# One transformer block on one core: query features scaled on one side only, written into padded rows at once; a new hand-written order with freely placed weight loads

## The chip, the cores and the metric

The kernel runs on one core of one Trainium2 chip. The metric is the device time of one execution in microseconds (us). TensorE (PE) multiplies matrices into PSUM, VectorE (DVE) and ScalarE (ACT) read PSUM and compute elementwise, GpSimd (POOL) computes elementwise on SBUF, and SyncE (SP) issues DMAs. ACT can issue DMAs too. Each engine works through its own list of instructions in order and waits on semaphores for the others.

## The reference

```python
def _A_ref(x, wqkv, w_phi, wo):                     # S = 2048, D = 640, H = 32, Dh = 20
    q, k, v = split(x @ wqkv)
    pq = einsum("bhsd,hdf->bhsf", q, w_phi)
    pk = einsum("bhsd,hdf->bhsf", k, w_phi)
    phi_q = concatenate([softmax(pq), softmax(-pq)], axis=-1)
    phi_k = concatenate([softmax(pk), softmax(-pk)], axis=-1)
    kv = einsum("bhsf,bhsd->bhfd", phi_k, v)
    z  = einsum("bhsf->bhf", phi_k)
    num = einsum("bhqf,bhfd->bhqd", phi_q, kv)
    den = einsum("bhqf,bhf->bhq", phi_q, z) + 1e-6
    return (num / den) @ wo
def _B_ref(x, w_gate, w_up, w_down):                # F = 1536
    return ((x @ w_gate) * (x @ w_up)) @ w_down
h = x + _A_ref(_layernorm(x), ...)
h2 = h + _B_ref(_layernorm(h), ...)
```

All inputs are bfloat16. The attention is linear: the sums over all keys (`kv`, `z`) must be complete before the first query can be divided.

## The kernel before, in words

The 2048 rows are 16 tiles of 128. For each tile t these operations exist, each with the name that the text uses (line numbers of the profile):

- **L1s, L1a, L1l, L1e, xn, xt**: first layer norm (L427 to L452) and the transposed tile, by PE for tiles 0 to 3 (L461), by a DMA transpose from SP's queue for the others (L470).
- **K, V, Q**: products of 128x640x640, ten matmuls of 320 columns each (L483). The feature matrix `w_phi` is folded into the K and Q weights first: WT (transposes of the K weights, L391), F1 and F0 (folds, L410), with their copies WTe, Fe1, Fe0 (L250).
- **Kx, Ks, Kr, Ke, Kn**: K features. Two ACT exponentials of 640 columns (plus and minus, L495), a DVE sum over 64 groups of 20 (L499), ACT `Ln` and `Exp` for the reciprocal (L502, L504), a POOL product over 1280 columns (L519).
- **KV**: eleven matmuls per tile that add up `kv` and `z` in PSUM (L527). After the last, **KVe** (L534) masks the result into `KVm`.
- **Qx, Qs, Qr, Qe, Qn**: the same for Q; POOL's Qn (L550, L554) scales all 1280 columns and writes them into rows of 11 blocks of 128 (`ph`). **qT** (L561) transposes these rows by DMA.
- **N**: numerator and denominator of a tile, twelve matmuls (L575), since block 5 is cut in two at a PSUM bank. **dd, rd, o** (L586, L588, L591) add 1e-6, take the reciprocal, and multiply. **oT** (L595) transposes, **O** multiplies by `wo` (L601), **h** adds `x` (L605).
- **L2s, L2a, L2v, L2r, hc, hT**: second layer norm, and its transpose by DMA (L628).
- **U, g, u, D, y, w**: the gated block in five groups of rows (256, 512, 512, 512, 256): gate and up products (L643), ACT copy (L648), DVE product (L651), down product (L662), residual (L674), store (L676). The first group, U0, needs tiles 0 and 1 only.

The order is written out by hand in a table, `PLAN`: per operation a key, a choice of engine where there are two, and buffer slots. Each engine runs its operations by rising key; the keys set the order only, and semaphores do the rest. `PACE` holds the weight loads behind the transposes of late tiles. PSUM has eight banks; a K, V, Q, N or O result takes two.

Around the change the orders are these. DMA issues at the start, all by SP: x0 w5 wk0 wk1 x1 wk2 x2 wk3 wk4 x3 wv1 wv0 wv2 x4 wv4 wv3 x6 x14 x8 x10 x12 (x of one or two tiles, wk and wv in fifths of 160 KB). Later: SP issues xt15 wg0 xt13 wo0 wu1 wu4 wo2 wd3 xt14 and seven more weights, ACT wg1 wu2 wd0. PE has finished eight Q products when the last KV ends; then come Q9 N1 N0 Q11 Q12 Q13 N2 Q14 N3 Q10 O1 O0 N5 Q8 N6 O2 Q7 N15 O3 N9 N4 and U0. SP, from the first transpose of an `o` tile to that of h tile 0: oT1 oT0 qT6 qT4 oT2 qT15 oT3 qT9 hT1 hT0.

Of the kernel before, what the change touches and what calls it, by code (L numbers as in the profile page):

```python
# [34 lines left out]
BW = [120 * g for g in range(10)] + [1152]  # L35
# [9 lines left out]
NSLOTS = {"psum": 8, "xn": 4, "ek": 7, "va": 8, "SR": 4, "ph": 4, "phT": 6, "o": 3, "oT": 4, "gt": 4, "hh": 2, "out": 3,  # L45
# [3 lines left out]
x0:0.7 w5:1.18:1 wk0:1.66:1 wv0:5.98:1 wk1:2.14 wv1:5.5 wk2:3.1:1 wv2:6.46:1 wk3:4.06 wv3:7.9 wk4:4.54:1 wv4:7.42:1 x1:2.62 x2:3.58 x3:5.02:1 x4:6.94  # L49
x6:8.38 x8:9.34 x10:9.82 x12:10.3 x14:8.86 wqt0:32.637 wqt1:35.357 wqt2:29.917 wqt3:27.197 wqt4:39.852 wo0:44.412 wo2:45.852 wd0:45.168:1 wd1:51.052  # L50
wd2:50.092 wd3:46.332 wg0:42.572 wu0:49.132 wg1:42.572:1 wu1:44.892 wg2:49.612 wu2:43.825:1 wg3:48.652 wu3:48.172 wg4:50.572 wu4:45.372 id0:2.41
gl0:0.7 eps:0.95 id1:2.93 gla0:3.77 glb0:4.21 gla4:2.19 glb4:3.33 gla1:1.97 glb1:3.55 gla2:4.43 glb2:4.85 gla3:2.71 glb3:3.99 va1:1.15 phz:6.025
mk0:4.65 mk1:5.07 mk2:5.775 mk3:6.925 mk4:7.325 zero:0.7 warm0:1.08::0 warm1:1.51 warm2:1.94 warm3:2.37 warm4:2.8 warm5:3.23 warm6:3.66 warm7:4.09
warm8:4.52 warm9:4.74 Ph0:4.717:1 Ph1:5.32 Ph2:4.36:1 WT0:4.96::1 WTe0:5.573:1 WT1:5.239::0 WTe1:5.788:1 WT2:6.114::3 WTe2:6.812:1 WT3:7.024::6
WTe3:8.16 WT4:7.725::7 WTe4:8.578:1 F1_0:6.394::4 Fe1_0:7.035:1 F1_1:6.709::0 Fe1_1:7.658 F1_2:7.41::2 Fe1_2:8.282:1 F1_3:8.763::0 Fe1_3:9.435
F1_4:9.387::6 Fe1_4:10.058:1 L1s0:3.021 L1a0:4.021 L1s1:5.992 L1a1:7.23 L1s2:7.34 L1a2:10.427 L1s3:8.997 L1a3:10.317 L1s4:10.537 L1a4:13.497
L1s5:11.357 L1a5:14.537 L1s6:13.607 L1a6:14.647 L1s7:12.177 L1a7:14.427 L1s8:19.637 L1a8:22.207 L1s9:16.397 L1a9:22.097 L1s10:14.757 L1a10:20.567
L1s11:15.577 L1a11:20.457 L1s12:25.657 L1a12:33.07 L1s13:30.22 L1a13:32.96 L1s14:29.4 L1a14:35.53 L1s15:33.18 L1a15:35.42 L1l0:4.311 L1e0:4.741
L1l1:8.905 L1e1:9.335 L1l2:10.717 L1e2:11.689 L1n2:12.199 L1n3:11.999 L1l4:14.996 L1e4:15.839 L1n4:16.349 L1n5:16.749 L1n6:16.149 L1n7:16.549
L1l8:23.514 L1e8:23.974 L1n8:24.884 L1n9:24.484 L1n10:24.684 L1n11:24.284 L1l12:35.85 L1e12:36.28 L1n12:37.279 L1n13:37.479 L1n14:36.879 L1n15:37.079  # L60
xn0:5.073::0 xt0:5.753::2 xte0:6.412 xn1:9.817::0 xt1:10.517::0 xte1:11.066 xn2:12.997::0 xt2:13.801::2 xte2:14.372 xn3:13.036:1:1 xt3:14.08::3
xte3:15.216 xn4:17.809:1:2 xt4:21.977 xn5:17.717::1 xt5:19.257 xn6:19.146:1:3 xt6:20.617 xn7:17.217::0 xt7:17.897 xn8:26.814:1:2 xt8:31.277
xn9:31.04::0 xt9:33.997 xn10:25.861:1:1 xt10:28.557 xn11:25.157::0 xt11:25.837 xn12:37.812::1 xt12:38.492 xn13:39.771:1:3 xt13:43.052 xn14:37.661:1:0
xt14:46.812 xn15:39.732::2 xt15:41.212 V0_0:9.115::2 V0_1:9.702 V0_2:10.245 V0_3:11.339 V0_4:11.611 Ve0:12.412::0 K0_0:8.004::4 K0_1:8.492 K0_2:9.973
# [12 lines left out]
Kn12:51.973 KV12:62.675 V13:51.405::0 Ve13:53.034::0 K13:49.504::2 Kx13_0:51.2::2 Kx13_1:52.033 Ks13:52.867::0 Kr13:54.472 Ke13:55.335 Kn13:56.691
KV13:69.782 V14:67.066::0 Ve14:69.077::2 K14:58.285::0 Kx14_0:60.33::1 Kx14_1:61.164 Ks14:61.997::1 Kr14:64.047 Ke14:64.497 Kn14:66.676 KV14:70.098
V15:61.317::4 Ve15:63.424::1 K15:47.515::4 Kx15_0:49.143::0 Kx15_1:49.977 Ks15:51.123::2 Kr15:52.723 Ke15:53.657 Kn15:54.332 KV15:70.413 KVe0:71.259
KVe1:70.999 F0_0:44.896::0 Fe0_0:45.648 F0_1:46.884::0 Fe0_1:47.469:1 F0_2:42.592::0 Fe0_2:43.823:1 F0_3:45.211::4 Fe0_3:46.272 F0_4:49.189::0  # L80
# [4 lines left out]
Qs4:69.287::1 Qr4:71.074 Qe4:71.937 Qn4:76.661::0 qT4:79.989::1 Q5:62.991::0 Qx5_0:64.647::3 Qx5_1:65.51 Qs5:66.344::2 Qr5:68.214 Qe5:69.7
Qn5:71.577::1 qT5:74.269::0 Q6:64.349::2 Qx6_0:66.134::4 Qx6_1:66.967 Qs6:67.8::0 Qr6:69.85 Qe6:70.3 Qn6:74.119::2 qT6:78.489::2 Q7:86.856::4
Qx7_0:88.485::2 Qx7_1:89.318 Qs7:110.524::0 Qr7:112.124 Qe7:112.574 Qn7:112.934::0 qT7:115.855::1 Q8:83.561::4 Qx8_0:85.19::0 Qx8_1:86.023
Qs8:101.317::1 Qr8:103.114 Qe8:103.66 Qn8:104.387::0 qT8:108.296::5 Q9:70.729::0 Qx9_0:72.357::0 Qx9_1:73.191 Qs9:76.05::2 Qr9:77.951 Qe9:78.814
Qn9:81.745::3 qT9:85.709::0 Q10:79.024::4 Qx10_0:80.652::6 Qx10_1:81.485 Qs10:91.885::0 Qr10:93.568 Qe10:94.114 Qn10:94.474::0 qT10:98.369::1
Q11:72.773::6 Qx11_0:74.414::1 Qx11_1:75.247 Qs11:77.66::0 Qr11:79.587 Qe11:80.451 Qn11:87.029::1 qT11:95.509::0 Q12:74.131::0 Qx12_0:75.871::3  # L90
Qx12_1:76.704 Qs12:95.909::1 Qr12:97.509 Qe12:98.164 Qn12:98.524::2 qT12:101.216::3 Q13:75.489::4 Qx13_0:77.327::4 Qx13_1:78.191 Qs13:80.622::1
Qr13:82.222 Qe13:82.672 Qn13:84.287::0 qT13:89.929::2 Q14:77.19::6 Qx14_0:78.964::5 Qx14_1:79.827 Qs14:99.435::0 Qr14:101.035 Qe14:101.485
Qn14:101.845::1 qT14:105.436::4 Q15:68.424::2 Qx15_0:70.45::2 Qx15_1:71.314 Qs15:72.147::3 Qr15:73.814 Qe15:74.264 Qn15:79.203::1 qT15:82.849::3
N0:72.43::2 dd0:73.757::1 rd0:74.247 o0:75.299::1 oT0:77.129::1 O0:81.86::6 h0:83.545 L2s0:85.117 L2a0:87.037 L2v0:89.571 L2r0:110.394 hc0:87.327::1
# [142 lines left out]
def build_graph():  # L237
# [662 lines left out]
```

## Time and profile before

| | before |
|---|---|
| median of 3 runs | 278.28 us (278.23 to 278.49) |
| the profiled execution | 276.56 us, of which its span 274.8 us |
| granted TensorE clock | 0.999 |
| PE, DVE, ACT, POOL busy | 266.0, 172.3, 113.2, 88.6 us |
| HBM read, written | 11.00 MB, 2.62 MB |

The span runs from the first to the last instruction; all times within the trace count from its start. Matmuls are pipelined: the time of one (299 ns for 320 columns) is a latency, and the rate is read from a long run of them. A group's idle time is the time that its engine had nothing to do just before it, with what ended that.

### The profile page before, as it was taken

The numbers are of one execution on the slowest core, as the hardware profiler recorded it, in microseconds if no ns is written. First come the engines' busy times: TensorE is split into PE (matmuls) and PEld (weight loads), VectorE is DVE, ScalarE is ACT, GpSimd is POOL, SyncE is SP. The second block draws the span as 40 slices with busy tenths as digits, with TensorE's granted clock in tenths as the row PEclk, the third lists the DMA queues.
The fourth block names the chain that finished last, engine by engine and source line by source line (L and its number), as shares of the span: only waits on it lengthen the run. The fifth ranks groups of instructions, "written<-read, shape, count | busy, mean of one in ns | idle before, by whom it ended". The sixth has DMA issues, their size and how long they took to land.

```text
span 274.8 us, 5227 instructions
## 1 busy us (share of the span) xinstructions
PE 266.0 (97%) x2119; PEld 176.7 (64%) x2119; DVE 172.3 (63%) x319; ACT 113.2 (41%) x240; POOL 88.6 (32%) x105
## 2 busy tenths in 40 slices
PE   7899999899999799999999999999999999999995
PEld 3676777677777587764455787665554467544773
DVE  5899999767789979987576337433365122323432
ACT  4899887678985444303242232003012310033000
POOL 7016999979998438240000000000000000000000
PEclk9999999999999999999999999999999999999999
DMA  6944758999689789867522100331002001100011
GB/s 167 317 144 95 98 110 174 302 294 341 141 147 176 146 141 186 163 74 160 52 47 49 26 0 2 84 50 48 25 2 48 0 0 50 52 0 2 24 48 57
DMA packets 66600, 27.77 MB, mean 101 GB/s; under 512 B 57744, under 2 KB 65296, under 8 KB 66576
## 3 DMA queue, kind: packets, MB, share of 16 engines
q1 hardware_dynamic: 65888, 26.15, 44.8%
q10 hardware_dynamic: 688, 1.28, 1.9%
q8 instruction: 17, 0.28, 0.4%
q14 instruction: 7, 0.06, 0.1%
HBM read 11.00 MB, written 2.62 MB: 50 GB/s over the span
## 4 chain that ended last, share of the span: by engine, by line
PE 84%; DMA 7%; DVE 4%; SPq 3%; issue 0%; DVEq 0%; ACT 0%
PE ps L643 34%; PE ps L483 22%; PE ps L662 17%; PE ps L601 7%; DMA xnT<-xn 3%; SPq L284 2%; PE ps L575 2%; DMA Wp<-in_A_wqkv_dram 2%; DMA scratch<-o 2%; DVE SR L499 2%; PE ps L527 1%; DMA out_dram<-Wp 1%; DVE o L591 1%; SPq L595 0%; DVE Wp L674 0%
## 5 line engine op out<-in xcount | busy, mean ns | idle before, releaser
L643 PE MATMUL ps<-xnT,Wgu 128*128 128x512 bf16 (+1 forms) x600 | 107.0, 336 | 1.2 <-DMA xnT<-xn 1.0
L643 PEld LDWEIGHTS ps<-xnT,Wgu 128*128 128x128 bf16 x600 | 58.0, 98 | 44.2 <-DVE ev L651 1.2
L648 ACT ACTIVATE gt<-ps 128x512 bf16<-128x512 f32 (+1 forms) x60 | 30.7, 512 | 101.9 <-PE ps L643 89.0
L483 PE MATMUL ps<-Wp,xnT 128*128 128x320 bf16 x480 | 69.0, 299 | 1.7 <-DMA xnT<-xn 1.3
L483 PEld LDWEIGHTS ps<-Wp,xnT 128*128 128x128 bf16 x480 | 45.2, 98 | 19.3 <-DMA xnT<-xn 1.8
L651 DVE TENSOR_TENSOR ev<-ps,gt 128x512 bf16<-128x512 f32 (+1 forms) x60 | 33.0, 577 | 37.6 <-PE ps L643 18.7
L662 PE MATMUL ps<-Wd,ev 128*128 128x320 bf16 (+2 forms) x396 | 53.2, 295 | 0.0
L499 DVE TENSOR_REDUCE SR<-ek 128x64 f32<-128x1280 bf16 x32 | 46.8, 1471 | 6.1 <-ACT ek L495 4.2
L495 ACT ACTIVATE ek<-ps 128x640 bf16<-128x640 f32 x64 | 43.3, 703 | 11.4 <-PE ps L483 10.1
L662 PEld LDWEIGHTS ps<-Wd,ev 128*128 128x128 bf16 x396 | 38.2, 98 | 14.9
L550 POOL TENSOR_TENSOR ph<-ek,SR 128x1200 bf16<-128x1200 bf16 x16 | 35.5, 2220 | 13.5 <-DMA scratch<-ph 7.4
L519 POOL TENSOR_TENSOR ek<-ek,SR 128x1280 bf16<-128x1280 bf16 x16 | 37.3, 2355 | 6.6 <-ACT SR L504 6.5
L674 DVE SCALAR_TENSOR_TENSOR Wp<-ps,rs,x_all 128x640 bf16<-128x640 f32 (+3 forms) x18 | 14.3, 805 | 35.5 <-PE ps L662 32.3
L615 POOL TENSOR_SCALAR ln<-mv 128x1 f32<-128x1 f32 x16 | 3.3, 209 | 87.2 <-DVE mv L614 87.2
L601 PE MATMUL ps<-Wo,scratch 128*128 128x320 bf16 x160 | 23.7, 299 | 0.2 <-DMA scratch<-o 0.2
L601 PEld LDWEIGHTS ps<-Wo,scratch 128*128 128x128 bf16 x160 | 15.3, 98 | 6.7 <-DVE ev L651 0.3
L605 DVE TENSOR_TENSOR x_all<-ps,x_all 128x640 bf16<-128x640 f32 x16 | 13.1, 816 | 3.7 <-PE ps L601 3.7
L624 ACT ACTIVATE xn<-x_all,mv 128x640 bf16<-128x640 bf16 x10 | 8.2, 825 | 16.5 <-DVE mv L614 16.5
L591 DVE TENSOR_TENSOR o<-ps,sm 128x640 bf16<-128x640 f32 x16 | 12.9, 814 | 1.5 <-DMA scratch<-o 1.0
L427 DVE BATCH_NORM_STATS2 st<-x_all 128x6 f32<-128x320 bf16 x16 | 7.7, 479 | 3.1 <-DMA x_all<-in_A_x_dram 3.0
L502 ACT ACTIVATE SR<-SR 128x64 f32<-128x64 f32 x32 | 8.1, 254 | 3.1 <-DVE SR L499 2.9
L575 PEld LDWEIGHTS ps<-KVm,scratch 128*128 128x128 bf16 x192 | 7.4, 98 | 2.9 <-DMA scratch<-ph 0.8
(54 smaller groups left out, 150.0 us busy)
## 6 DMA issues: line engine op xcount, KB each, us to landing
out_dram<-Wp SPq DMA_DIRECT2D x15, 160.0 KB, 1.8
x_all<-in_A_x_dram SPq DMA_DIRECT2D x6, 320.0 KB, 6.0
Wgu<-in_B_w_gate_dram SPq DMA_DIRECT2D x4, 384.0 KB, 7.5
Wgu<-in_B_w_up_dram SPq DMA_DIRECT2D x4, 384.0 KB, 8.5
Wd<-in_B_w_down_dram SPq DMA_DIRECT2D x3, 480.0 KB, 10.9
scratch<-in_A_wqkv_dram SPq DMA_DIRECT2D x5, 160.0 KB, 3.2
Wp<-in_A_wqkv_dram SPq DMA_DIRECT2D x5, 160.0 KB, 4.7
x_all<-in_A_x_dram SPq DMA_DIRECT2D x4, 160.0 KB, 3.4
```

Source lines behind the costliest of these rows:

```text
L483: ins = e.matmul(pb(b, hb)[:, 0:320], lhsT=T["xnT"][:, NC - 1 - c, P * t:P * (t + 1)], rhs=T["Wp"][:, POS[kind], c, 320 * hb:320 * (hb + 1 ...
L495: G.op("act", "%sx%d_%d" % (nm, t, s), lambda e, s=s, b=b, ek=ek: e.activation(out=T["ek"][:, ek.slots[0], :].rearrange("p (b h s f) -> p ...
L499: G.op("dve", "%ss%d" % (nm, t), lambda e, ek=ek, sr=sr: e.tensor_reduce(out=T["SR"][:, sr.slots[0], 0, :], in_=T["ek"][:, ek.slots[0], :] ...
L519: G.op("pool", "Kn%d" % t, lambda e, ek=ek, sr=sr: e.tensor_tensor(out=T["ek"][:, ek.slots[0], :].rearrange("p (h f) -> p h f", f=DH), in0 ...
L550: e.tensor_tensor(out=o_[:, 0:10 * P].rearrange("p (g n) -> p g n", n=P)[:, :, 0:120].rearrange("p g (h f) -> p g h f", f=DH), in0=i_[:, 0 ...
L591: G.op("dve", "o%d" % t, lambda e, sm=sm, b=b, o=o: e.tensor_tensor(out=T["o"][:, o.slots[0], :].rearrange("p (b h d) -> p b h d", b=2, d= ...
L601: ins = e.matmul(pb(b, hb)[:, 0:320], lhsT=T["oT"][:, oT.slots[0], c, :], rhs=T["Wo"][:, c, 320 * hb:320 * (hb + 1)], start=(c == 0), stop ...
L643: ins = e.matmul(pb(b)[:, 0:n], lhsT=T["Wgu"][:, gu, c, P * ft:P * (ft + 1)], rhs=T["xnT"][:, NC - 1 - c, o0:o0 + n], start=(c == 0), stop ...
L648: G.op("act", "g%d_%d" % (bi, ft), lambda e, pg=pg, gt=gt, n=n: e.activation(out=T["gt"][:, gt.slots[0], 0:n], in_=pb(pg)[:, 0:n], func=AF ...
L651: o_ = G.op("dve", "u%d_%d" % (bi, ft), lambda e, pu=pu, gt=gt, hh=hh, ft=ft, n=n: e.tensor_tensor(out=T["hh"][:, hh.slots[0], ft, 0:n], i ...
L662: ins = e.matmul(pb(b, hb)[:, 0:w], lhsT=T["hh"][:, hh.slots[0], ft, P * tt:P * (tt + 1)], rhs=T["Wd"][:, ft, c0 + w * hb:c0 + w * (hb + 1 ...
L674: return e.scalar_tensor_tensor(out=o, in0=i0, scalar=T["rs2"][:, t:t + 1], in1=i1, op0=ALU.mult, op1=ALU.add)
```

## The change

1. **Q features.** Per head and side, e is the exponential and S its sum. Before, both sides were divided by their own S. Now the plus side stays as it is and the minus side is multiplied by S+/S-. Numerator and denominator then both carry a factor S+, and the 1e-6 in the denominator is multiplied by S+ (dd), so the quotient is the same. Qr still takes logarithms of the sums; a new POOL operation **Qb** subtracts them (32 columns); Qe takes the exponential of 32 columns; Qn multiplies 660 columns in place where it had 1200 and 80.
2. **Padded rows at once.** Qx writes straight into the rows of eleven blocks of 120 (+8). Each side takes three ACT instructions (300, 300 and 40 columns) where it took one of 640. Q products are cut at column 300 and not 320. Qs sums 66 groups (1320 columns) and not 64.
3. **Eleven numerator products.** N's result is cut at head 18, so no block is cut in two: eleven matmuls per tile and not twelve. dd, rd and o run over 36 heads (720 columns) and not 32 (640).
4. **Buffers.** `ek` has 5 slots and not 7 (K alone uses it), `ph` has 6 and not 4, sums have their own tile `S`; `oT`, `wkn` and `zero` move into other tiles' space; small POOL memsets are added or changed; the warm-up matmuls write eight banks.
5. **Weights placed freely.** `PACE` is gone, and the table is new for all operations.

```diff
-BW = [120 * g for g in range(10)] + [1152]
+BW = [120 * g for g in range(NB)]
...
-        ek, sr = feat("Q", t, b, kk)
...
+        for sg in range(2):
+            def qx(e, sg=sg, b=b, ph=ph):
+                v = pv(ph).rearrange("p g (j s f) -> p g j s f", s=2, f=DH)[:, :, :, sg, :]
+                i0, i1 = pb(b, 0)[:, 0:300], pb(b, 1)[:, 0:300]
+                for o_, i_ in ((v[:, 0:5], i0), (v[:, 5:10], i1)):
+                    e.activation(out=o_, in_=i_.rearrange("p (g j f) -> p g j f", j=3, f=DH), func=AF.Exp, scale=1.0 - 2.0 * sg)
+                return e.activation(out=v[:, 10, 0:2], in_=pb(b, 1)[:, 300:340].rearrange("p (j f) -> p j f", f=DH), func=AF.Exp,
+                                    scale=1.0 - 2.0 * sg)
...
+            return e.tensor_tensor(out=T["RQ"][:, rq.slots[0], 1, 0:32].unsqueeze(2), in0=l_[:, :, 0:1], in1=l_[:, :, 1:2],
+                                   op=ALU.subtract)
...
+            v = pv(ph).rearrange("p g (j s f) -> p g j s f", s=2, f=DH)[:, :, :, 1, :]
+            return e.tensor_tensor(out=v, in0=v, in1=T["RQ"][:, rq.slots[0], 1, 0:33].rearrange("p (g j) -> p g j", j=3).unsqueeze(
+                3).to_broadcast([P, NB, 3, DH]), op=ALU.mult)
...
-                for h0, h1 in [(3 * g, 3 * g + BH[g])] if g != 5 else [(15, 16), (16, 18)]:
-                    y = h0 // 16
+                y, h0, h1 = g // 6, 3 * g, 3 * g + BH[g]
...
-            for o_ in PACE[t]:
-                o_.before.append(G.by["xt%d" % t])
```

The orders that the new table gives, for the same places as above:

- DMA issues at the start, by SP: x1 w5 wk2 wk1 wv1 x6 wv2 wv3 wv4 x10 wu0 wu3 wu1 wqt3; by ACT: x0 wk0 x3 x2 wk3 wk4 x4 wv0 x12 x8. x14 comes later.
- ACT, from its first copy to the last copy of a folded K weight: WTe0 L1l0 WTe2 L1l1 L1e0 WTe1 L1e1 Fe1_2 Fe1_0 Fe1_1 WTe4 L1l2 Fe1_3 L1e2 Fe1_4. PE behind that last copy and ahead of its third tile of K or V: K1 and K0 (a fifth each), xt3, V1 (four fifths), V0 (whole); xt2 follows.
- SP in the middle: wo0 xt10 xt8 xt9 wg0 xt11 wo2 wd0 wg4 wu4 wg3 wg1 wd3 xt13 wg2 xt15 xt12 wd1 xt14 wd2 qT3. No weight is issued by ACT. PE, from about the issue of xt13 to its first use: K8 K11 Q0 Q3 KV6 KV7 V9 K10 Q1 KV8 V10, then K13.
- PE has finished ten Q products when the last KV ends; then come Q7 N1 N3 N0 Q11 Q8 N2 Q14 N9 O1 O0 Q12 N5 O3 Q15 N4 N7 O2 O9 and U0.
- DVE behind KVe: Qs6 dd1 dd0 rd1 rd0 dd3 o0 o1 (before: Qs15 dd1 dd0 rd1 rd0 o1 o0). POOL ahead of the last KV: Qb5 Kn15 Qn5 Qb4 Kn14 (Kn14 is needed by KV14). SP: qT4 (its slot is free once N1 has run), qT13 (once N3 has run), then oT1 oT0 qT10 oT3 qT7 oT2 oT9 hT1 hT0.

More of the change, by code (lines that the diff above doesn't have):

```diff
@@ L48 @@
 for _t in """
[L49 to L56, printed above, removed]
@@ L61 @@
[L61 to L64, printed above, removed]
@@ L77 @@
[L77 to L80, printed above, removed]
@@ L85 @@
[L85 to L92, printed above, removed]
```

307 lines of the change are left out of this document (171 added, 136 removed).

## The prediction

> **What bounds the kernel now.** I read, in this order, the busy shares and the chain by engine, PE's waits (engine, line, what it waited for: us, times, longest), and PE's timeline (start, duration, and in brackets the idle time before with what ended it).
>
> ```profile
> PE 266.0 (97%) x2119; PEld 176.7 (64%) x2119; DVE 172.3 (63%) x319; ACT 113.2 (41%) x240; POOL 88.6 (32%) x105
> ...
> PE 84%; DMA 7%; DVE 4%; SPq 3%; issue 0%; DVEq 0%; ACT 0%
> ```
>
> ```profile
> PE ps L483 <- DMA xnT<-xn: 1.3, 1, 1.3
> ...
> PE ps L643 <- DMA xnT<-xn: 1.0, 1, 1.0
> ...
> PE ps L483 <- DMA Wp<-in_A_wqkv_dram: 0.4, 1, 0.4
> PE ps L575 <- DMA scratch<-ph: 0.3, 1, 0.3
> ```
>
> ```profile
> 5.12 0.72 PE L391 MATMUL ps<-ident,scratch 128*128 128x128 bf16 x10
> ...
> 51.27 0.48 PE L410 MATMUL ps<-Phi,scratch 128*128 128x140 bf16 x6
> ...
> 53.04 5.61 PE L483 MATMUL ps<-Wp,xnT 128*128 128x320 bf16 x40 [1.30 <-DMA xnT<-xn]
> ...
> 73.43 1.18 PE L527 MATMUL ps<-ev,ek 128*128 128x63 bf16 x33
> ...
> 96.01 9.45 PE L643 MATMUL ps<-xnT,Wgu 128*128 128x256 bf16 x85 [1.04 <-DMA xnT<-xn]
> ...
> 254.07 17.45 PE L662 MATMUL ps<-Wd,ev 128*128 128x320 bf16 x132
> ```
>
> PE bounds it. Its longest waits in real work are for DMAs, and none stands behind 96.01, where the gated block (U0) begins and PE runs to 254.07 + 17.45 = 271.52. So three places can give time back: the start (from 5.12, behind the warm-up), the wait that ends at 53.04, and the stretch from the last KV (end 73.43 + 1.18 = 74.61) to U0: 21.4 us, a chain that PE must fill with other products. POOL, which the change relieves most, is at 32% and on no piece of the chain.
>
> Prices of PE's work, from the chain's pieces in order of time:
>
> ```profile
> 16.15 15.78 PE ps L483 x116
> ...
> 73.59 1.01 PE ps L527 x33
> ...
> 75.97 0.71 PE ps L575 x24
> ...
> 112.29 2.72 PE ps L601 x20
> ```
>
> A 320-column matmul is 15.78/116 = 0.136, so a K, V or Q product 1.36; a KV 1.01/3 = 0.34; an N 0.71/2 = 0.355; an O 1.36.
>
> **Part 1, the start.** The third tile of K or V begins at 16.15 plus four matmuls, 16.69. Before it, the V weights were late, as the chain's pieces and the table of 5 us windows (busy time of PE, PEld, DVE, ACT, POOL, then clock, DMA share, GB/s) show:
>
> ```profile
> 0.79 0.40 SPq L284
> ...
> 8.00 4.93 DMA Wp<-in_A_wqkv_dram
> ```
>
> ```profile
> 5.00:10.00 5.00, 4.10 (x60) 3.31 (x57) 4.59 (x12) 3.50 (x7) 0.85 (x5) 1.00 0.92 282
> 10.00:15.00 5.00, 4.58 (x42) 3.09 (x39) 4.20 (x12) 4.44 (x9) 0.50 (x2) 1.00 1.02 336
> ```
>
> The last V weight is SP's sixteenth DMA, one each 0.48 us from 0.79 on, issued at 8.00 and landed at 12.93. In these windows the DMAs move 282 and then 336: issue is the limit until 10. Afterwards two engines issue, and the V weights stand before most of x. SP's ninth DMA carries the last one: 0.79 + 8 x 0.48 = 4.6 issued, with the same 4.93 landed at 9.5. The wait for it goes; the first tiles are then set by ACT's copies.
>
> The Trainium skill, "DMA: Bandwidth & Descriptors", section "Issuing engines are not separate DMA queues", says that a second issuing engine saves only the sequencer's time, for all run on the same 16 engines. The trace agrees in that 336 GB/s is not far above the 282 of one issuer. By it the 18 loads of 160 KB up to this weight (2.9 MB, both queues) need 8.8 us at 336 GB/s, so it lands some 2 us later than the 9.5 above, and the gain is smaller at its lower bound, not in the middle that is taken below, which ACT's copies set.
>
> ```profile
> L866 ACT ACT_TABLE_LOAD x1 | 1.3, 1283 | 0.8 <-PEq L885 0.8
> ```
>
> ```profile
> 5.87 0.70 ACT L250 ACTIVATE scratch<-ps 128x640 bf16<-128x640 bf16 x1 [1.09 <-PE ps L391]
> ...
> 7.32 1.30 ACT L250 ACTIVATE Wp<-ps 128x640 bf16<-128x640 f32 x2
> ...
> 9.98 0.20 ACT L438 ACTIVATE rs<-ln 128x1 f32<-128x1 f32 x1
> ```
>
> Two copies take 1.30, one 0.70, so each adds 0.60. ACT's new list up to the last folded K weight has nine copies (5.4) and six small ones (0.15 to 0.2 each, 1.0). It can begin at about 5.6 (the first transposes run from 5.12 to 5.4) and ends at 12.0; behind it PE has eleven fifths of a product (0.27 each, 3.0) and two times five transposes (0.28 each): 15.7, or 1.0 early. But ten DMA issues stand ahead of this list on ACT's queue. If they begin behind the table load, which ends at 0.8 + 1.3 = 2.1, ten at 0.45 make it 6.6, and of the gain nothing is left. I take the middle: **-0.5**, bounds -1.0 to +0.6 (the longer POOL memsets ahead of the fold's factors are in the upper one).
>
> **Part 2, the middle.**
>
> The chain's piece, and the issues of ACT and SP from their timelines:
>
> ```profile
> 44.95 8.05 DMA xnT<-xn
> ```
>
> ```profile
> 43.04 0.41 ACTq L284 DMA_DIRECT2D Wgu<-in_B_w_gate_dram  x1
> ...
> 44.32 0.58 SPq L284 DMA_DIRECT2D Wgu<-in_B_w_gate_dram  x1
> ...
> 49.65 4.66 SPq L470 DMA_TRANSPOSE xnT<-xn  x1
> ```
>
> K13 waits for xt13, which lands 8.05 after its issue, since weights share the DMA engines with it. PE's last fold before it was over at 51.27 + 0.32 = 51.59, so 1.45 is lost. In the new order seven loads (2.98 MB) stand just ahead of xt13, more than before; but eight products and three KV lie between its issue and K13, 8 x 1.36 + 3 x 0.34 = 11.9 us. At 8.05 it is in time; the cover would have to be beaten by 3.9. xt8, xt9 and xt7 have less cover and only one load near. I take **-1.2** (1.45, with 0.25 given back there), bounds -1.45 and +2.2 (second rival).
>
> **Part 3, two more Q products before the last KV.** Ten and not eight: +2.72 at the end of KV, and as much less to fill the chain with. The end of KV moves to 74.61 - 0.5 - 1.2 + 2.72 = 75.6.
>
> **Part 4, the chain from KV to U0.** SP's timeline, and the minimum, median and maximum of one qT issue in ns:
>
> ```profile
> 76.72 2.47 SPq L561 DMA_TRANSPOSE scratch<-ph  x1
> ```
>
> ```profile
> 79.23 2.60 SPq L595 DMA_TRANSPOSE scratch<-o  x2
> ...
> 91.78 2.80 SPq L628 DMA_TRANSPOSE xnT<-xn  x2
> ```
>
> ```profile
> L561 SPq DMA_TRANSPOSE scratch<-ph x16: 1263/1458/3040, 64.6 to 121.4; - x16
> ```
>
> SP issues without a pause from oT1 at 79.23 to the end of hT1 and hT0 at 91.78 + 2.80 = 94.58: ten issues, 1.53 each. This queue sets the chain's end, with hT0 in front of U0 (the wait of 1.0 above). Afterwards nine stand there: 13.8, that is -1.5. But oT1 itself starts later: DVE has dd3 and o0 (0.81) ahead of o1, and qT4 and qT13 can only be issued once N1 and N3 have run, where before the issue in front of oT1 started at 76.72, bound to none of the N's. With Q7 and N1 (1.7) and two issues of 1.4 to 2.4 it begins 4.6 to 6.6 after KV; before 79.23 - 74.61 = 4.62. The ends are 0 and +2.0; nearer the median issue I take +0.7. Sum **-0.8**, a chain of 20.6; bounds 19.8 (oT1 as early as before, rounded) and 22.9 (oT1 at +2.0, and +1.0 for the waits below). U0 starts at 75.6 + 20.6 = 96.2 (before 96.01).
>
> **Part 5, what is left behind U0.** 11 O and 8 N, where it was 12 and 7: -1.36 + 0.34 = **-1.0**. All of it runs without a gap, so PE ends at 271.5 + 0.2 - 1.0 = 270.7.
>
> **Prices that do not reach the sum**, from the groups by line and shape (busy us, mean ns of one, idle before):
>
> ```profile
> L495 ACT ACTIVATE ek<-ps 128x640 bf16<-128x640 f32 x64 | 43.3, 703 | 11.4 <-PE ps L483 10.1 <-PE ps L527 0.4
> ...
> L648 ACT ACTIVATE gt<-ps 128x256 bf16<-128x256 f32 x24 | 9.2, 384 | 18.8 <-PE ps L643 13.5 <-DVE ev L651 5.1
> ...
> L550 POOL TENSOR_TENSOR ph<-ek,SR 128x1200 bf16<-128x1200 bf16 x16 | 35.5, 2220 | 13.5 <-DMA scratch<-ph 7.4 <-ACT SR L504 6.1
> ...
> L554 POOL TENSOR_TENSOR ph<-ek,SR 128x80 bf16<-128x80 bf16 x16 | 5.1, 318 | 0.0
> ...
> L499 DVE TENSOR_REDUCE SR<-ek 128x64 f32<-128x1280 bf16 x32 | 46.8, 1471 | 6.1 <-ACT ek L495 4.2 <-POOL ek L519 1.7
> ...
> L591 DVE TENSOR_TENSOR o<-ps,sm 128x640 bf16<-128x640 f32 x16 | 12.9, 814 | 1.5 <-DMA scratch<-o 1.0
> ```
>
> Qx: on the line through 256 and 640 columns (0.83 ns a column) 300 columns are 0.42 and 40 are 0.20. Consecutive ones overlap by 0.1, so three add 0.74 where one added 0.60: +0.14, over 32 of them 4.5 us of ACT, at 41%. Bounds 0 (the extra starts vanish) and +0.4 a side (no overlap at all): it frees the PSUM pair that O0 takes, 0.8 for both sides at most. Qn by columns: 2.22 x 660/1200 = 1.22 to 1.31; with Qb (at most L554's 0.32) POOL gains 0.9 a tile that nobody waits for. But Qb is a new wait on POOL: it stands for Qr, and so for the sum before it; behind Qb4 in POOL's list stands Kn14, for which KV14 and the last KV wait. Nearest is the wait of POOL for ACT in L550's row, 6.1 in two times; of this I count 0 (Qr4 is done, the likelier, as its products lie some 10 us ahead) and with O0's 0.8 allow +1.0 in the bound above. Qs grows by 1471 x 40/1280 = 46 ns, o by 814 x 80/640 = 0.1; two o's in the chain are inside its bounds. N's eleventh saves 0.355 - 0.34 = 0.02 a tile, 0.2 in all, which I leave as margin.
>
> **Sum.** -0.5 - 1.2 + 2.72 - 0.8 - 1.0 = -0.8 on the span of 274.8 (its execution: 276.56). The median of the runs is 278.28, 1.7 above that execution; the difference carries over: **277.5**, own range 276.6 to 278.1.
>
> **Rivals.**
>
> *Everything comes off* (0.10). Start -1.0, middle -1.45, chain 19.8: a further -0.5 - 0.25 - 0.8, **276.0**. For it: none of these waits is one of PE's own work. Against: each needs its lower bound.
>
> *The chain does not shorten* (0.14). SP's gain of one issue is spent in the wait for N1 and N3; 21.4 again, +0.8: **278.3**, no change. For it: the 2.47 of the issue before oT1, and a maximum of 3.04 in the list.
>
> *Transposes sit behind the freely placed weights* (0.22). Slower, at one place: xt13 behind seven loads. xt14 before, behind eight loads, blocked SP for 4.66 and landed 10.9 after its issue, the longest of its line:
>
> ```profile
> DMA to landing us min/median/max: 2.6/2.7/10.9
> ```
>
> Those loads had been issued over 5 us, the new ones over 3.4 us, so xt13 could need 10.9 + 1.6 to 3.2, 12.5 to 14.1 against a cover of 11.9. It decides from 11.9 on; at 14.1 the middle is -1.45 + 2.2 = +0.75 and not -1.2, which gives **279.4**. The same Trainium skill page, section "Queues, rings and completion order", says that each DMA engine consumes one issuer's descriptors in the order of their ring; by it a transpose on SP's ring lands behind all weights issued ahead of it there, which speaks for this rival, as no weight goes by ACT any more.
>
> *PE runs dry in the chain* (0.16). Six Q's are left to fill it and not eight. If the two issues before oT1 and the Qx of three instructions take their upper ends, the chain is 22.9: +2.3, **279.8**. Against: nine issues stand where ten stood.
>
> **How the numbers follow.** The forecast has 0.38. A measurement of this kernel tells 0.2%, 0.56 us, from no change. Of the forecast's range three quarters lie below that line (0.31), of the unshortened chain's a small part on either side (0.02). Faster: 0.10 + 0.31 + 0.02 = 0.43. Within: 0.07 + 0.10 = 0.17. Slower: 0.22 + 0.16 + 0.02 = 0.40. The range of 8 in 10 goes from 275.9 to 280.8.
>
> **What would show it.** Right: PE's wait for xnT at K13 gone; the last V weight landed by 10 to 12; last KV near 75.6; nine issues from oT1 to hT0; U0 near 96.2. Wrong: a new wait of PE for xnT between 25 and 60 (the weights), or U0 past 97.0, from where the sum turns. Wrong too if PE shows waits behind U0.

## The result and the profile after

| | before | after |
|---|---|---|
| median of 6 runs | 278.25 us (277.80 to 279.26) | 273.91 us (273.63 to 274.75) |
| ratio | | 0.9844, 95% interval 0.9823 to 0.9865 |
| profiled execution, span | 276.56, 274.8 us | 273.93, 272.2 us |

The changed kernel is 4.3 us faster. 0.8 was forecast, with a range down to 275.9: the direction was right, the size was not. "Faster" had been given 0.43 and "slower" 0.40, so the direction was forecast with little confidence. Of the 4.3, 2.6 lie between the two profiles (276.56 and 273.93). The other 1.7 is the distance of before's median from its own profile; after's median and profile are equal.

The page of after, busy shares and chain:

```profile
PE 266.0 (98%) x2103; PEld 177.2 (65%) x2103; DVE 171.0 (63%) x315; ACT 116.6 (43%) x307; POOL 73.9 (27%) x107
...
PE 93%; ACT 3%; DMA 2%; ACTq 1%; issue 0%; DVE 0%; DVEq 0%
```

PE's waits of after (engine, line, what it waited for: us, times, longest):

```profile
PE ps L371 <- DVE ev L366: 1.2, 1, 1.2
PE ps L482 <- ACT ph L554: 0.8, 1, 0.8
PE ps L392 <- DMA ev<-in_A_wqkv_dram: 0.8, 3, 0.4
PE ps L411 <- ACT scratch L251: 0.5, 1, 0.5
PE ps L616 <- ACT RQ L567: 0.3, 1, 0.3
```

No wait for a transpose (xnT, `scratch<-ph`, `scratch<-o`) is left; in the list of before the two for xnT stood first and third. Between KV and U0 there are two waits for ACT in their place: 0.8 for the exponentials of Qx (`ph`) and 0.3 that the profile puts down to Qe (`RQ`). PE's timeline has the marks of the prediction: the last KV, the first product of U0, and the last run of products:

```profile
74.65 1.52 PE L526 MATMUL ps<-ev,ek 128*128 128x63 bf16 x44
...
95.74 4.43 PE L658 MATMUL ps<-xnT,Wgu 128*128 128x256 bf16 x39
...
252.20 17.45 PE L677 MATMUL ps<-Wd,ev 128*128 128x320 bf16 x132
```

KV ends at 74.65 + 1.52 = 76.17, U0 begins at 95.74, and PE ends at 269.65. Cut at these marks, the table of windows (start and end, length, PE's busy time, clock, DMA share, GB/s) gives for before:

```profile
0.00:17.00 17.00, 14.45 (x127) 1.00 0.82 252
17.00:74.61 57.61, 56.25 (x568) 1.00 0.81 186
74.61:96.01 21.40, 19.91 (x228) 1.00 0.90 149
96.01:271.52 175.51, 175.39 (x1200) 1.00 0.28 53
271.52:274.80 3.28, 0.00 (x1) 0.94 0.20 65
sum 274.80, PE 266.01; mean PE 53.20
```

and for after:

```profile
0.00:17.00 17.00, 14.48 (x122) 1.00 0.95 305
17.00:76.17 59.17, 59.16 (x593) 1.00 0.91 184
76.17:95.74 19.57, 18.43 (x199) 1.00 0.78 135
95.74:269.65 173.91, 173.91 (x1195) 1.00 0.26 51
269.65:272.20 2.55, 0.01 (x1) 1.00 0.26 84
sum 272.20, PE 265.99; mean PE 53.20
```

The reader is to look at the last line first: PE's work is 266.0 us in both. What was moved (two Q products ahead of KV, one O product, one N) cancels. The whole difference between these two profiles is PE's idle time, length minus busy, stage by stage: 2.55 and 2.52 up to 17 us, 1.36 and 0.01 up to KV, 1.49 and 1.14 up to U0, 0.12 and 0 behind it, 3.28 and 2.54 in the tail. That is -0.03 - 1.35 - 0.35 - 0.12 - 0.74 = -2.6.

Theory for the experiments: the gain is waits for DMAs that the new order and the smaller program remove, some of which the profile of before did not show; POOL's relief and the eleven products give PE nothing by themselves. Rivals: POOL's relief gives the gain; what is taken away in the middle comes back ahead of U0; the start is set by ACT's issues or by the K weights.

### The profile page after: what moved, and what is told of

The parts are those of the page before. It is cut to its first block, busy times and chain, and to the rows that moved or that the text cites. A ratio compares the mean times of both kernels' runs of the same rounds, so it can differ in the third digit from the quotient of the medians.

```text
span 272.2 us, 5234 instructions
## 1 busy us (share of the span) xinstructions
PE 266.0 (98%) x2103; PEld 177.2 (65%) x2103; DVE 171.0 (63%) x315; ACT 116.6 (43%) x307; POOL 73.9 (27%) x107
## 4 chain that ended last, share of the span: by engine, by line
PE 93%; ACT 3%; DMA 2%; ACTq 1%; issue 0%; DVE 0%; DVEq 0%
PE ps L658 38%; PE ps L482 23%; PE ps L677 19%; PE ps L616 8%; DMA ev<-in_A_wqkv_dram 2%; PE ps L526 2%; ACT ph L553 2%; PE ps L589 1%; PE ps L411 1%; ACTq L285 1%; PE ps L462 0%; ACT ph L554 0%; PE ps L392 0%; ACT L884 0%; DVE Wp L689 0%
## 5 line engine op out<-in xcount | busy, mean ns | idle before, releaser
L482 PE MATMUL ps<-Wp,xnT 128*128 128x320 bf16 (+1 forms) x480 | 68.6, 299 | 0.8 <-ACT ph L554 0.8
L553 ACT ACTIVATE ph<-ps 128x300 bf16<-128x300 f32 x64 | 23.8, 442 | 7.9 <-PE ps L482 7.4
L557 DVE TENSOR_REDUCE S<-ph 128x66 f32<-128x1320 bf16 x16 | 24.2, 1515 | 3.1 <-ACT ph L554 3.1
L498 DVE TENSOR_REDUCE SR<-ek 128x64 f32<-128x1280 bf16 x16 | 23.4, 1472 | 1.3 <-ACT ek L494 1.2
L616 PE MATMUL ps<-Wo,Wp 128*128 128x320 bf16 x160 | 23.9, 299 | 0.3 <-ACT RQ L567 0.3
L494 ACT ACTIVATE ek<-ps 128x640 bf16<-128x640 f32 x32 | 22.3, 714 | 2.7 <-PE ps L482 2.4
L571 POOL TENSOR_TENSOR ph<-ph,RQ 128x660 bf16<-128x660 bf16 x16 | 20.9, 1307 | 6.2 <-ACT RQ L567 6.2
L639 ACT ACTIVATE xn<-x_all,mv 128x640 bf16<-128x640 bf16 x13 | 10.7, 828 | 24.2 <-DVE mv L629 24.2
L616 PEld LDWEIGHTS ps<-Wo,Wp 128*128 128x128 bf16 x160 | 15.2, 98 | 6.6 <-issue 0.6
L606 DVE TENSOR_TENSOR o<-ps,sm 128x720 bf16<-128x720 f32 x16 | 14.2, 894 | 0.1
```

The costliest lines, as they stand in the source:

```text
L482: ins = e.matmul(pb(b, hb)[:, 0:n1 - n0], lhsT=T["xnT"][:, NC - 1 - c, P * t:P * (t + 1)], rhs=T["Wp"][:, POS[kind], c, n0:n1], start=(c = ...
L494: G.op("act", "%sx%d_%d" % (nm, t, s), lambda e, s=s, b=b, ek=ek: e.activation(out=T["ek"][:, ek.slots[0], 0:2 * D].rearrange("p (b h s f) ...
L498: G.op("dve", "%ss%d" % (nm, t), lambda e, ek=ek, sr=sr: e.tensor_reduce(out=T["SR"][:, sr.slots[0], 0, :], in_=T["ek"][:, ek.slots[0], 0: ...
L553: e.activation(out=o_, in_=i_.rearrange("p (g j f) -> p g j f", j=3, f=DH), func=AF.Exp, scale=1.0 - 2.0 * sg)
L557: G.op("dve", "Qs%d" % t, lambda e, t=t, ph=ph: e.tensor_reduce(out=T["S"][:, t, 0:66].rearrange("p (g k) -> p g k", k=6), in_=pv(ph).rear ...
L571: return e.tensor_tensor(out=v, in0=v, in1=T["RQ"][:, rq.slots[0], 1, 0:33].rearrange("p (g j) -> p g j", j=3).unsqueeze(3).to_broadcast([ ...
```

## The experiments

Each run was timed beside the kernel before on its chip. That kernel's median was 278.42 us beside the second profile of before, the moved transposes, the output slot and POOL's 660 columns; 279.37 beside the mended kernel before, the new code in the old order and the first two runs on the start; 278.36 beside the mended new code, the changed kernel run again, POOL's 420 columns and the mixture at the start; 277.84 beside the two runs with twelve products. Medians of different groups are therefore compared through their ratios to it.

**Before, profiled again.** No edit.

> The kernel before, unchanged, profiled a second time. Its first profiled execution took 276.56 us, its median of six runs is 278.25; the changed kernel's profiled execution (273.93) equals its median (273.91). Theory A: the 1.7 between them is time that a usual run of before loses in waits for DMAs which the first profile did not show, so a second profile comes near 278 and has a wait of PE that is longer by 1 to 2 us, in the middle (the wait of K13 for its transpose, 1.3 in the first) or at the start. Theory B: it is a constant of profiling (the span plus a fixed overhead), so a second profile takes 276.6 again, with the same waits within 0.3 us.

279.0 us, span 277.3. PE's waits:

```profile
PE ps L410 <- DMA scratch<-in_A_wqkv_dram: 2.1, 1, 2.1
...
PE ps L483 <- DMA Wp<-in_A_wqkv_dram: 1.1, 1, 1.1
```

The 1.1 belongs to the start, where the first profile had 0.4. The 2.1 is new: the first fold of a Q weight waits for the last transposed Q weight (wqt4). The chain of waits shows its landing:

```profile
41.49 5.43 DMA scratch<-in_A_wqkv_dram
46.92 0.24 issue
47.16 0.48 PE ps L410 x6
```

In the first profile the same transpose landed 3.5 us after its issue at 40.85, so at 44.35, and the fold ran at 44.56 with no wait: 0.2 us were to spare. K13's wait, the 1.30 of the first profile, is absent here, since PE comes later by the other wait. The tail, too, is longer, 4.05 (below). Stage by stage PE idles 3.14, 2.06, 1.45, 0.77 and 4.05 us, where the first profile had 2.55, 1.36, 1.49, 0.12 and 3.28. Behind U0, 0.5 of the 0.77 is a wait for DVE; the other growth is waits for DMAs. Theory A holds on this one execution: a run of before can wait for DMAs at places that another profile does not show.

**Transposes of tiles 13 and 14 ahead of the late weights.** The kernel before with

```diff
-xt13:43.052 xt14:46.812 wg1:42.572:1 wu2:43.825:1 wd0:45.168:1
+xt13:42.56 xt14:42.565 wg1:47:1 wu2:47.1:1 wd0:47.2:1
```

> The kernel before with one edit of order: the transposes of tiles 13 and 14 are issued ahead of all late weights, and the three weights that ACT issued go some 4 us later. Theory (the wait of 1.3 to 1.45 us at K13 is all that the middle could give): the wait goes, the profile is 1.2 to 1.5 shorter than that of before and the median 1.2 to 1.5 lower (276.8). Rival 1 (the usual run of before waits longer there than its profile showed): the median falls by 2.5 to 3.2 (275.4). Rival 2 (a wait removed here comes back in the chain between the last KV and U0, since SP's transposes set its end): the median falls by under 0.5.

277.37 us (274.83 to 278.48), ratio 0.9957 (0.9928 to 0.9986), -1.05 on this chip. K13's wait is gone, and KV to U0 is 21.36, as before, so nothing of it came back ahead of U0. But the profile, forecast 1.2 to 1.5 shorter, has a span of 275.8, 1.0 longer than the first one of before: a wait of 0.9 for an early transpose (at 23.7 us) and one of 0.5 at the Q fold stand in the middle, and its idle time there is 1.38, as in the first profile (1.36; 2.06 in the second). The median is about a microsecond lower; that K13's wait is what it lost is not shown by this profile.

**The output slot.** The kernel before with

```diff
-y13_0:265.609::0
+y13_0:265.609::2
```

> The kernel before with one edit: the residual of tile 13 goes to output slot 2 and not 0, so it does not wait for the store of tile 12. Theory (the tail of before, 3.3 us from PE's end to the span's end, holds a wait for that store, which the changed kernel no longer has): 0.7 to 0.9 less, the tail 2.5 us. Rival (the last store is held by the DMA queue anyway, so that the wait is cover): within 0.2 of before.

276.24 us, ratio 0.9893 (0.9834 to 0.9952), tail 2.5. The row of DVE's waits in before that the edit takes away is

```profile
DVE Wp L674 <- DMA out_dram<-Wp: 3.2, 1, 3.2
```

The wait for the store in the tail is real. With the shared slot the three profiles of the old code so far have tails of 3.28, 3.59 and 4.05, so it costs 0.75 to 1.5. The median fell by 2.2, at least 1.3 by the interval (0.48% of 278.4), over the 0.7 to 0.9 that was expected; whether all of that is the tail, four runs do not show.

**The three covers mended.** The kernel before with both edits above and

```diff
-wqt4:39.852
+wqt4:38
```

> The kernel before with three covers mended and nothing else: the last transposed Q weight is issued ahead of the transpose of tile 12 (the first Q fold waited up to 2.1 us for it, and not at all in the first profile), the transposes of tiles 13 and 14 ahead of the late weights, and the residual of tile 13 in output slot 2. Theory (the usual run of before loses about 1.4 at the fold, 1.1 at K13 and 0.9 to 1.5 in the tail, and these are most of the 4.3 us): the median is 274.6 to 275.6, and the three waits are gone from the profile. Rival (waits that are removed in the middle come back ahead of U0, where transposes set the end): 276.5 to 277.5.

275.21 us (274.48 to 276.42), ratio 0.9865 (0.9814 to 0.9915). The windows between 17 us and the last KV, and the tail:

```profile
17.00:74.22 57.22, 56.63 (x570) 1.00 0.76 187
...
270.73:273.30 2.57, 0.00 (x1) 1.00 0.26 85
```

The three waits are gone (0.5 for an early transpose is what is left in the middle). The old code with six keys and a slot changed gets most of what the whole change gets; its interval contains the 0.9844 of the changed kernel. The rival falls: KV to U0 took 20.6 here, not longer.

**The new code in the old order.** All keys of before; Qb 0.3 behind Qr, Qe put off to stand behind Qb, and buffers as below:

```diff
-NSLOTS = {... "ek": 5, ... "ph": 6, ...}
+NSLOTS = {... "ek": 7, ... "ph": 7, ...}
```

> The code of the changed kernel (half scaling, padded rows, eleven numerator products) in the order of before: every operation has its old key, and Qb stands behind Qr. K keeps seven exponential buffers and the padded rows get seven, so that no new wait for a buffer comes in. Theory (the gain is the order: loads and transposes placed so that nothing waits for them, and the tail's slot; the arithmetic alone gives nothing that PE sees): 277.6 to 278.8, level with before. Rival (POOL's relief of 15 us and the one pass less are worth time by themselves, the padded rows being ready earlier): 276.5 or less. Second rival (Qe now waits for Qb in POOL's list, so that the order of before cannot take the new code): 279.5 to 282.

277.43 us, ratio 0.9938 (0.9906 to 0.9971). The theory's band was level with before, and it came 1.9 lower. From where, the marks say: KV ends at 74.94, where before had 74.61 in its first profile and 75.75 in its second, which has a wait at the Q fold like this one (1.8 here, 2.1 there); U0 is at 96.80, so KV to U0 takes 21.86 (21.40 and 21.35); behind U0 PE has 174.93 us and no gap, 0.6 less than in the first profile; the tail is 2.57, 0.7 less. PE's idle time between 17 us and KV is that one wait (1.78). So POOL's relief shortened nothing ahead of U0, and the chain is longer by 0.5: PE waits 1.1 and 0.6 there for ACT's exponentials (Qx), which it did not in before. What the code gives is behind U0 and in the tail, and the tail was a surprise, because y13 still shares its slot here.

**The new code in the old order, mended.** The same, with xt13, xt14, wqt4 and ACT's three weights as in the mended kernel before.

> The new code in the old order with the covers mended as in the mended kernel before (last transposed Q weight earlier, transposes of tiles 13 and 14 ahead of the late weights). Theory (what the arithmetic gives is the shorter N and the store in the tail only, about 1 to 1.7, and the mended covers add to it): 275.0 to 276.0, and the rest down to the changed kernel, 1 to 2 us, is the rest of the new order (ten Q products ahead of KV, nine transposes in the chain). Rival (the mended covers are all of it, and code and order cancel): 273.8 to 274.6.

275.13 us (275.00 to 275.82), ratio 0.9900 (0.9844 to 0.9956), within the theory's band. This is the plainest test of the arithmetic: with the covers mended, old code (0.9865) and new code (0.9900) cannot be told apart, and their profiles have spans of 273.3 and 273.2 us. On this chip the changed kernel itself, run again, took 274.43 (273.87 to 274.68), ratio 0.9864 (0.9826 to 0.9903):

> The changed kernel, unchanged, profiled and timed again beside the next three on one chip. Theory (it loses its waits for DMAs for good, so that its runs differ little): the median is 273.6 to 274.2, all runs within 1.2 us of each other, the profile again has PE idle for under 0.3 us between the third tile and the last KV, and none behind U0.

Its profile has no PE idle between 17 us and KV and its runs lie within 0.8 us, while before's lie from 276.5 to 280.3 on the same chip. So beyond the mended covers the new order is worth another 0.7 us here, below the 1 to 2 expected. The median of 274.43 is 0.2 above its own band.

**POOL's load put back.** The changed kernel with one more product per tile ahead of Qn, of 660 columns in the first run, 420 in the second:

```diff
+        def qd(e, t=t, ph=ph):
+            v = pv(ph).rearrange("p g (j s f) -> p g j s f", s=2, f=DH)[:, :, :, 1, :]
+            return e.tensor_tensor(out=v[:, 0:7], in0=v[:, 0:7], in1=T["S"][:, t, 64:65].unsqueeze(2).unsqueeze(3).to_broadcast([P, 7, 3, DH]), op=ALU.mult)
+        G.op("pool", "Qd%d" % t, qd, pool_c(660), LP, [ph, rq, S_b[t]], [ph], kk)
```

> The changed kernel with one more POOL product per tile (660 columns, the minus half times ones, just ahead of Qn), so that POOL carries about 16 x 1.3 = 21 us more than in the changed kernel (some 95 us, over the 88.6 of before). Theory (the lighter POOL work is on nobody's path): at most 0.5 us over the changed kernel, 273.9 to 274.4. Rival (the gain of 4.3 us comes in good part from POOL's relief, through Qn ahead of the transposes and Kn ahead of the last KV): 1.5 to 4 us over it, 275.4 to 278, with new waits of SP or PE for POOL between the last Q and U0.

284.63 us, ratio 1.0191 (1.0123 to 1.0259): some 10 over the changed kernel, far past the rival too.

> The changed kernel with a POOL product of 420 columns per tile just ahead of Qn (the minus half of seven blocks, times ones), 16 x 0.9 = 14.4 us: as much as the change took from POOL (88.6 to 73.9). Theory (ten Q products ahead of the last KV fit only because POOL was relieved; the new order cannot be had with the old POOL load): 5 to 8 us over the changed kernel, 279 to 282, so that the change would be a loss without the relief. Rival (the 10.7 us of the larger load came from its last third, beyond the old load): at most 3 over it, 277 or less.

279.87 us, ratio 1.0061 (1.0032 to 1.0090), 5.4 over the changed kernel on that chip: with the POOL load of before the new order, as it stands, is a loss. KV ends at 80.15 and not 76.27, and KV to U0 takes 21.21 and not 19.77. ACT's waits in the changed kernel and in this one, in this order:

```profile
ACT RQ L567 <- POOL RQ L564: 1.1, 2, 0.8
```

```profile
ACT RQ L567 <- POOL RQ L564: 11.4, 10, 2.3
```

This is the new wait of ACT for Qb. Behind it on ACT stand the exponentials of the next tiles; PE's waits in the second run:

```profile
PE ps L482 <- ACT ph L554: 2.9, 2, 2.6
PE ps L482 <- ACT ek L494: 1.9, 2, 1.2
...
PE ps L526 <- POOL ek L518: 1.1, 1, 1.1
```

Windows of 5 us (busy time of PE, PEld, DVE, ACT, POOL) say why, first the changed kernel, then the one with 420 columns:

```profile
65.00:70.00 5.00, 5.00 (x39) 3.57 (x37) 4.04 (x4) 3.91 (x14) 5.00 (x4) 1.00 0.74 159
70.00:75.00 5.00, 5.00 (x48) 3.66 (x46) 4.65 (x5) 3.41 (x16) 5.00 (x6) 1.00 0.56 105
75.00:80.00 5.00, 4.20 (x86) 3.53 (x83) 4.54 (x10) 3.51 (x16) 3.41 (x5) 1.00 0.19 38
```

```profile
65.00:70.00 5.00, 4.33 (x33) 2.91 (x31) 3.84 (x4) 3.74 (x13) 4.92 (x6) 1.00 0.68 129
70.00:75.00 5.00, 3.75 (x27) 2.25 (x26) 2.02 (x3) 2.75 (x11) 4.92 (x5) 1.00 0.46 88
75.00:80.00 5.00, 3.95 (x64) 3.13 (x63) 3.98 (x4) 3.18 (x15) 4.92 (x6) 1.00 0.39 74
```

POOL is at 27% over the span, but at 86% from 17 us to the last KV (50.8 of 59.2 us), full from 65 to 75 us even in the changed kernel, and at 68% from 75 to 80, as KV ends. My theory ("on nobody's path") falls in this form. The relief alone moves nothing (the new code in the old order), but this order, with ten Q products ahead of KV, needs it. Whether another order could carry the old load was not tried.

**The start.** The changed kernel, ACT issuing six DMAs and not ten:

```diff
-x4:3.58:1 x8:5.02:1 x12:4.54:1 wv0:4.06
+x4:3.58 x8:5.02 x12:5.4 wv0:4.06:1
```

> The changed kernel with six DMA issues on ACT's queue at the start and not ten (x4, x8, x12 and one V weight go to SP). Theory (ACT's ten issues hold its first copy until 6.46, and its copies set the start): the first copy begins at about 5.6, the third tile 0.4 to 0.8 earlier, the median 273.1 to 273.5. Rival (the K weights that land late set the start, whatever ACT does): no change, 273.7 to 274.1.

274.27 us (273.68 to 274.76), ratio 0.9825 (0.9782 to 0.9868), no change that can be told. ACT's first copy does begin earlier, 5.81 and not 6.46, but the last K weight lands at 10.18 and not 9.85, and PE now waits for the K weights, 1.7 us where it was 0.8:

```profile
PE ps L392 <- DMA ev<-in_A_wqkv_dram: 1.7, 3, 0.8
```

The five K weights ahead of x2 and x3:

```diff
-wk1:2.14 wk3:2.62:1 wk4:3.1 x2:2.14:1 x3:1.66 L1l2:10.546
+wk1:1.66:1 wk3:2.14 wk4:2.14 x2:3.1:1 x3:2.62 L1l2:11.56
```

> The changed kernel with the five K weights issued ahead of x2 and x3. Theory (ACT's issues set the start): no change, 273.7 to 274.2. Rival (the last K weight lands at 9.85 and holds its transpose, its copy and the fold): it lands by 8, the third tile comes 0.8 to 1.2 earlier, the median is 272.8 to 273.2. Bound above: tiles 2 and 3 come later with their x, +0.5.

275.35 us (274.78 to 276.32), 1.1 above the run with six issues on the same chip. The K weights land by 7.5, but tiles 2 and 3 are late, and KV ends at 77.02 (76.17). A mixture, six issues on ACT and the K weights only partly ahead:

```diff
-wk3:2.62:1 x3:1.66 wk4:3.1 x2:2.14:1 L1l2:10.546
+wk3:1.66:1 x3:2.14 wk4:2.62 x2:3.1:1 L1l2:11.5
```

> The changed kernel with six DMA issues on ACT and not ten, and the K weights ahead of x2 (but not all ahead of x3), with the second layer norm step of tiles 2 and 3 placed accordingly. Theory (the start is set by two things that cover each other, ACT's issues and the K weights' landing, so each alone gives nothing): with both eased the third tile comes 0.4 to 0.8 earlier and the median is 273.1 to 273.6. Rival (the DMA engines' rate sets the start: what lands earlier makes something else late): 273.9 to 274.8, with a new wait for x2 or x3.

273.96 us (273.34 to 274.75) beside 274.43 for the changed kernel on that chip; their runs overlap, so a gain can't be told. PE waits for a K weight (0.8) and for tile 3 (0.4) in it. Until 17 us the DMA engines move 302 to 308 GB/s in all of these, before 252: neither ACT's issues nor the K weights alone set the start, and what lands earlier makes something else late.

**Twelve numerator products.** The new code in the old order, and the changed kernel, with

```diff
-                y, h0, h1 = g // 6, 3 * g, 3 * g + BH[g]
+                y = g // 6
+                for h0, h1 in [(3 * g, 3 * g + BH[g])] if g != 5 else [(15, 16), (16, 18)]:
```

> The new code in the old order with block 5 of the numerator cut in two again (twelve products per tile, 16 matmuls more). Theory (the change's sixteen matmuls fewer save a seventeenth block of TensorE's program, whose load made the store of the tile next to last late): a seventeenth load of 16 KB comes back near 269 to 272, a store there lands 3 us or more after its issue and not 1.8, the tail from TensorE's end to the span's end grows from 2.5 to 3.3 to 4.0, and the median is 0.8 to 1.8 above the same order with eleven (277.43), 0.3 of it the products themselves. Rival (the late store has another cause in the old code): the store lands in 1.8, the tail stays 2.5, the median is 0.2 to 0.5 above.

The list of DMA queues (packets, MB, share) in the new code with eleven, then with twelve products:

```profile
q8 instruction: 16, 0.26, 0.4%
```

```profile
q8 instruction: 17, 0.28, 0.4%
```

The old code has 17 as well. With twelve products the chain of waits of the tail reads

```profile
268.09 0.89 DVE Wp L701
268.99 0.02 issue
269.00 4.07 DMA out_dram<-Wp
273.07 0.03 issue
273.09 0.03 DVE Wp L701
```

The store takes 4.07 where the three stores before it and the one behind it take 1.8, the last residual waits for it, and the tail is 4.27 (2.57 with eleven). The block is loaded from 270.1 to 271.8, while the store is under way. The median, 277.47 (275.02 to 279.26, ratio 0.9950, 0.9903 to 0.9998), does not show it: the Q fold's wait, 1.9 here, varies as much from run to run. The profile shows the cause, the median does not show its price (the ratios with eleven and twelve products, 0.9938 and 0.9950, overlap).

> The changed kernel with twelve numerator products. Theory (the same block comes back, but no residual waits for that store): a seventeenth load near 266 to 270, one late store, the tail 2.5 unless the late store is one of the last two; the median 0.2 to 0.5 above the changed kernel (274.1 to 274.9), the price of 16 products. Rival: the tail grows by 0.7 or more here too, 275 to 276.

274.78 us (274.36 to 275.23), ratio 0.9843 (0.9779 to 0.9907), tail 2.52. The seventeenth block is back and makes one store late, 3.4 us, but nobody waits for its slot. PE has 0.34 more behind U0: by the starts of its matmuls 0.16 are the eight products there, 0.02 each, and 0.17 is one pause ahead of an N at 115.8 us.

## Why the prediction was off

**Right**: PE bounds the kernel; the waits of K13 and in the chain are for DMAs and go; the weights ahead of xt13 do not make it late (it was issued at 39.74 and landed 9.9 later, over the 8.05 that was taken and right behind the last of the seven loads ahead of it, at 49.09, but within the 11.9 of cover, so the rival of the transposes behind the weights fell); nine issues stand from oT1 to hT0. U0 came at 95.74, forecast 96.2, but in part by luck, since two errors cancel: KV ended 0.57 later than forecast (76.17 and 75.6), and the chain was 1.03 shorter.

**The carry-over, the largest error (1.7).** "The difference carries over": this step of the sum failed. I took the 1.7 between before's profile and its median as fixed. It is mostly waits for DMAs, at the Q fold, at the start and in the tail, which change from run to run. The second profile shows them, the mended kernel removes those at the fold and in the tail, and the changed kernel does not have these two: its median equals its profile. What was missing is the cover of each DMA that PE does not wait for, the time from its issue to its use: at the fold it left 0.2 us to spare, while the landing took 3.5 in one run and 5.4 in another.

**The tail (0.74).** I took what lies behind PE's end as the same, without a reason. The row was in the list of DVE's waits, shown with the output slot: y13 starts 3.2 idle behind the store of tile 12. It goes by two ways, each enough alone: a slot of its own (late store of 3.9, tail 2.53) and a program shorter by one block (shared slot, tail 2.57).

**The chain (1.0 of 1.8).** Forecast 20.6, measured 19.57, against 21.40. SP's queue in after:

```profile
81.13 2.79 SPq L610 DMA_TRANSPOSE Wp<-o  x2
...
91.74 2.60 SPq L643 DMA_TRANSPOSE xnT<-xn  x2
```

oT1 was issued 4.96 behind KV (taken 5.3), and the nine issues took 13.2 (taken 13.8). The sign of the error could have been seen: with +2.72 ahead of KV, -0.8 in the chain and -1.0 behind U0, moved work did not cancel, so that the sum contained 0.9 of new PE idle time that no row gave. The chain's work fell by 1.48 (19.91 to 18.43), its idle time from 1.49 to 1.14. Of the 1.14, 0.8 and 0.3 are the new waits for ACT; the prediction had the 0.8 in its bound and nothing in its sum. hT0 lands at 95.69, just ahead of U0: PE's work and SP's queue now end together.

**The middle.** -1.2 was sized a little low; PE's idle time there fell by 1.35.

**Behind U0.** -1.0 was taken, -1.6 measured (175.51 to 173.91). Of the rest the eleven products are 0.16 (0.02 each, as the prediction priced them for its margin), and 0.33 are two pauses between matmuls of before, at 108 and 125 us, that after does not have; 0.1 I can't place. The new code in the old order, where nothing is moved, has the same 0.6 less.

**The start.** -0.5 forecast, nothing measured: the third tile, the 41st matmul of K and V, starts at 16.80 in before and at 16.81 in after (the 16.69 of the prediction counts four matmuls where six stand, and its sum for after has both groups of transposes ahead of the mark, where one follows it). Idle time up to 17 us is the same (2.55 and 2.52). ACT's copies begin at 6.46 behind its issues, as the upper bound said, but partly by luck: the issues ran beside the table load from 0.81 and took up to 0.98 each, not ten of 0.45 from 2.1. The last K weight lands only at 9.85. The last V weight landed at 12.7 and not 9.5. The rule that I set beside it, from the Trainium skill, "DMA: Bandwidth & Descriptors", section "Issuing engines are not separate DMA queues", was nearer: 2 us later than 9.5. The 282 and 336 GB/s compared there are both of one issuer; up to 17 us one issuer moved 252 GB/s in before and two moved 305 in after.

**POOL.** "POOL gains 0.9 a tile that nobody waits for" fits the old order, where with the relief PE's idle time up to KV was still a wait for a DMA and the chain did not shorten, though three Qn stand on the chain that ended last in the second profile of before (80.3 to 87.4 us). It is wrong as a statement on the change: 5.4 us hang on it in the new order. The share of the span hid a stretch in which POOL is 86% busy, and two windows in which it is full.

## What to carry to other kernels

- Where PE's work is constant, write the sum as a ledger of PE's idle time by stage; moved work must cancel in it, and a remainder is an error or a wait that needs a row.
- Ask of every DMA that feeds the bounding engine how much cover it has, also where the profile shows no wait. Here a median above the profiled run was the sign of covers with nothing to spare, and mending them needed six keys and a slot.
- Read an engine's load in the windows where its consumers wait, not over the span, before calling its relief worthless.

## What the runs showed of the hardware

A change of sixteen matmuls in TensorE's program reached a store at the end. Loads of 16 KB of instructions come by a queue of their own (q8), each taking about 1 us of one DMA engine (0.9 to 2.4 in these traces; 17 x 1 us is the 0.4% of sixteen engines' 275 us that the queue's row shows). That they are TensorE's is read from the pair whose only edit is these matmuls. Seventeen occur with 2119 matmuls, sixteen with 2103. The seventeenth is loaded at 268 to 271 us, beside the store of 160 KB, which then lands 3.1 to 4.1 us after its issue. This held in each of seven profiles with 17 loads, and in none of nine with 16 was a store there later than 1.8. It is not a matter of the last store alone: in the seven profiles of the changed order with 16 loads, one store in the middle (issued at 180.67 in the changed kernel) lands 3.4 to 3.8 us after its issue, and a load of q8 begins 0.65 to 1.2 us behind its issue each time (at 181.31 in the changed kernel). All fourteen stores over 3 us in the sixteen profiles met such a load, which began 0.65 to 1.72 us behind the issue; none of the stores issued when a load was already under way took more than 2.2. The Trainium skill, "Runtime: NRT & Kernel Launch", section "Instruction fetch mechanics", says that programs are refilled in blocks of 16 KiB, and that the cost of crossing a boundary is mostly hidden. The size agrees with the trace. The cost was hidden for TensorE, but not for the transfer that the load met. Why a load of 1 to 1.7 us costs the store up to 2.3 stays open.
